# A turn of a quarter in place of a squared half angle: h·cos h between two matmuls, with the order of tasks written anew

## Chip, cores and metric

One core of one Trainium2 chip. The time is device microseconds of one execution; 929.7 us is the median of three runs of the kernel before (925.52 to 930.39).

## What is computed

Attention over 4 batches, 8 heads, 576 positions, head size 64: softmax attention on q, k, v averaged by fours, repeated four times, plus softmax attention within a band of |i-j| < 4. Its output x, 2304 rows of 512, goes through two multilayer products:

```
h = x @ w_in          # 512 -> 2048
g = h * cos(h)
y = g @ w_out         # 2048 -> 512
out = ((y @ w_a) * (y @ w_b)) @ w_out2   # 512 -> 1536 -> 512
```

All inputs are float32 (some arrive as 64-bit words and are converted on the core). Each factor of a large product is split into a rounded part and the rest, and a product is three matmuls: high·high, high·low, low·high (`mm3`, L577 to L579).

## The kernel before

Tokens are cut into 8 units of 288 for attention and into 7 stretches (five of 288 columns, two of 432) for the first product pair. A **group** g is one stretch with one of the 16 blocks of 128 hidden features; there are 112. Per group: `h{g}.0..3` (four `mm3` of x with w_in into one of two PSUM banks called `h`), `c{g}.0..6` (the cosine, function `cosine`, L624 to L645), `b{g}.0..3` (four `mm3` with w_out into `acc0` to `acc3`). Because the banks number two, a group's first matmul waits until the group two places earlier in the order has left its bank. That happens at the step that multiplies by h, L639.

The cosine before, per group: ScalarE rounds h/2π to an integer (L628), VectorE subtracts that many turns from h (L630), ScalarE takes the sine of half the rest (L632), ScalarE (L635) or VectorE (L637) squares it and doubles it, VectorE forms (1 - that)·h (L639). Then follow a rounded copy `gh` (L293 or L295) and the rest `gl` (L645), which the back matmuls read.

All of this and the attention (`sm` to `xl`: scores L384 and L408, maxima, exponentials L430/L437/L440, sums, transposes L476/L489, products L504/L511, the sum of both parts L527, the split into `xbig` L293/L295/L551) and the conversion of weights (`w{t}.0..4`: ScalarE L276 and L279, VectorE L281, copy L293/L295, rest L570) is written in one string, `ORDER`. A word such as `c5.1@d` is a task and its engine (a ScalarE, d VectorE, p GpSimd); each engine's instructions, and the queue of loads, run in the order of that string. ScalarE has one function table for exponentials and one for sines; a change is an ACT_TABLE_LOAD. After the string come the last products (`z`, L577 to L579 too), whose order is made by loops that the change leaves alone.

Of the kernel before, what the change touches and what calls it, by code (L numbers as in the profile page):

```python
# [48 lines left out]
L0w7 w7.0@a w7.1@a xl0.1@p h1.0 h1.1 h0.1 ln0.1 lz0.1@d L0s3 vs0.3@d L0w5 vs0.2@p L0w6 dt0.1 w4.4@p w3.1@a w3.2@d dc0.1@a w3.3@d lt0.1 lc0.10@a
lc0.11@a at0.1 Lc8 w5.0@a w5.1@a w5.2@d up0.1@a cb0.3 Lc13 w6.1@a w3.4@p cb0.2 xh0.3@a xh0.2@d xl0.2@d xl0.3@d w6.0@a w6.2@d lp1.0 w8.0@a Lq1.3 w5.3@a  # L50
w7.2@d w5.4@p h0.2 h0.3 c0.0@a c0.1@d w6.3@a h1.2 h1.3 c1.0@a lm1.0 Lc9 w6.4@p c0.2@a c0.3@a c1.1@d c1.2@a w7.3@d lu1.0@p dp1.0 c0.4@d c0.5@d h2.0
h2.1 h2.2 lu1.1@p w8.1@a c1.3@a h2.3 dx1.0 da1.00@d c0.6@p b0.1 Lq1.2 c1.4@d c1.5@d h3.0 h3.1 h3.2 h3.3 da1.01@d b0.0 w9.0@a w8.2@d lp1.1 sm1.3@d b0.3
w8.3@d b0.2 sm1.2@p c1.6@p b1.2 b1.3 b1.1 le1.0 ln1.0 Lc14 c2.0@a c2.1@d b1.0 lm1.1 Lc11 w11.0@a c3.0@a de1.0 c3.1@d w9.1@a w9.2@d w8.4@p dp1.1 dn1.0
lz1.0@p lu1.2@p Lq2.2 c2.2@a c2.3@a c3.2@a c2.4@d Lc10 w10.0@a dx1.1 da1.10@d h4.0 h4.1 da1.11@d dz1.1@p lu1.3@p Lc22 c2.5@a c2.6@p c3.3@a c3.4@d
c3.5@d h4.2 h4.3 w11.1@a w7.4@d dz1.0@p w10.1@a Lw2.0 lt1.0 lc1.00@d w9.3@d Lc27 c4.0@a c4.1@d lc1.01@d w10.2@d b2.2 Lc21 de1.1 b2.1 w11.2@d c3.6@p
dn1.1 w11.3@d Lq2.0 h5.0 h5.1 h5.2 Lk2.1 h5.3 c5.0@a c5.1@d L0V le1.1 ln1.1 dt1.0 b2.0 Lc12 w10.3@d w9.4@p b2.3 dc1.0@a at1.0 up1.0@d cb1.0 cb1.1
# [1164 lines left out]
```

## Time and profile before

| | |
|---|---|
| median of three runs | 929.7 us (925.52 to 930.39) |
| the profiled execution | 928.92 us, span 927.1 us |
| busy: TensorE, VectorE, ScalarE, GpSimd | 891.7, 705.2, 576.2, 509.2 us |
| mean granted TensorE clock | 0.987 |

PE is TensorE's matmuls, PEld its weight loads, DVE VectorE, ACT ScalarE, POOL GpSimd. A row of groups names line, engine, operation, tile written and tiles read, shapes, count, then busy time and mean of one in ns, then the idle time of the engine just before and what ended it. A matmul's end is modelled, so its row is longer than the step to the next one.

### The profile page before, as it was taken

The page shows a single profiled execution, that of the slowest core. Times are in us where ns is not written, and L with a number is a line of the kernel's source. Part 1 is how long each engine was busy: PE and PEld are TensorE (multiplying, and loading weights), DVE is VectorE, ACT ScalarE, POOL GpSimd, SP SyncE. Part 2 cuts the span into 40 slices and gives each one's busy share as a digit, 9 for nine tenths or more (in the row PEclk, how much of TensorE's full clock was granted, in tenths as well). Part 3 has the DMA queues.
Part 4 walks back from the last instruction along what each step waited for, and adds up shares of the span by engine and source line. Part 5 has one row for each costly group of instructions (what it writes and reads, how often), then busy time and mean ns, then how long its engine had stood idle before and what let it go on. Part 6 is the DMA issues. An engine that isn't in the chain of part 4 may idle for free.

```text
span 927.1 us, 18811 instructions
## 1 busy us (share of the span) xinstructions
PE 891.7 (96%) x6828; PEld 864.4 (93%) x6828; DVE 705.2 (76%) x1332; ACT 576.2 (62%) x1249; POOL 509.2 (55%) x654
## 2 busy tenths in 40 slices
PE   4688999999999999999999999999999999999998
PEld 2588999999999999999998999999999999999998
DVE  6899998797687876855666697869768677776764
ACT  5797988566486785743575555557644566544473
POOL 4566766455166655631545177656576753677540
PEclk9788999999999999999999999999999999999999
DMA  9775432254475755400787454594743366832641
GB/s 260 249 262 183 144 122 84 79 152 134 146 226 156 233 164 175 144 1 24 227 288 204 147 199 156 177 384 183 281 176 112 106 236 244 333 105 72 219 160 52
DMA packets 97581, 162.12 MB, mean 175 GB/s; under 512 B 6736, under 2 KB 63568, under 8 KB 97488
## 3 DMA queue, kind: packets, MB, share of 16 engines
q1 hardware_dynamic: 97488, 160.92, 52.3%
q8 instruction: 54, 0.88, 0.4%
q14 instruction: 39, 0.32, 0.1%
HBM read 127.66 MB, written 33.23 MB: 174 GB/s over the span
## 4 chain that ended last, share of the span: by engine, by line
PE 81%; DVE 10%; ACT 3%; issue 3%; POOL 2%; DMA 0%; SPq 0%; POOLq 0%; DVEq 0%; ACTq 0%
PE z L578 14%; PE z L577 14%; PE z L579 14%; PE acc L577 6%; PE h L577 6%; PE acc L578 6%; PE acc L579 6%; PE h L579 5%; PE h L578 5%; DVE raw L281 1%; PE att L384 1%; DVE gs L639 1%; PE att L511 1%; PE att L476 1%; PE att L504 1%
## 5 line engine op out<-in xcount | busy, mean ns | idle before, releaser
L968 POOL TENSOR_TENSOR sb<-w,sb 128x256 fp32r<-128x256 f32 x154 | 125.2, 826 | 115.5 <-ACT sb L966 110.5
L577 PE MATMUL h<-xbig,w 128*128 128x288 f32 (+1 forms) x448 | 147.0, 328 | 8.4 <-DVE gs L639 8.3
L577 PE MATMUL acc<-gh,w 128*128 128x288 f32 (+1 forms) x448 | 144.1, 322 | 0.0
L579 PE MATMUL h<-xbig,w 128*128 128x288 f32 (+1 forms) x448 | 142.2, 317 | 0.0
L578 PE MATMUL h<-xbig,w 128*128 128x288 f32 (+1 forms) x448 | 141.9, 317 | 0.0
L578 PE MATMUL acc<-gl,w 128*128 128x288 f32 (+1 forms) x448 | 141.0, 315 | 0.7 <-DVE gl L645 0.7
L579 PE MATMUL acc<-gh,w 128*128 128x288 f32 (+1 forms) x448 | 140.8, 314 | 0.0
L966 ACT ACTIVATE sb<-w 128x256 fp32r<-128x256 f32 x252 | 97.0, 415 | 53.0 <-PE z L579 44.3
L577 PEld LDWEIGHTS h<-xbig,w 128*128 128x128 f32 x448 | 86.2, 192 | 14.2 <-DVE gs L639 11.2
L645 POOL TENSOR_TENSOR gl<-gs,gh 128x288 fp32r<-128x288 f32 (+1 forms) x61 | 59.4, 980 | 69.9 <-ACT gh L293 35.0
L577 PE MATMUL z<-xbig,sb 128*128 128x384 f32 x288 | 97.3, 338 | 0.0
L579 PE MATMUL z<-xbig,sb 128*128 128x384 f32 x288 | 97.2, 337 | 0.0
L578 PE MATMUL z<-xbig,sb 128*128 128x384 f32 x288 | 97.1, 337 | 0.0
L628 ACT ACTIVATE gs<-h 128x288 int32<-128x288 f32 (+1 forms) x112 | 49.4, 441 | 64.5 <-PE h L579 60.3
L577 PEld LDWEIGHTS acc<-gh,w 128*128 128x128 f32 x448 | 85.0, 190 | 3.6 <-issue 1.2
L579 PEld LDWEIGHTS h<-xbig,w 128*128 128x128 f32 x448 | 86.3, 193 | 1.0
L578 PEld LDWEIGHTS h<-xbig,w 128*128 128x128 f32 x448 | 86.2, 192 | 1.0
L578 PEld LDWEIGHTS acc<-gl,w 128*128 128x128 f32 x448 | 85.0, 190 | 1.9 <-DVE gl L645 0.9
L579 PEld LDWEIGHTS acc<-gh,w 128*128 128x128 f32 x448 | 84.9, 190 | 1.0
L630 DVE SCALAR_TENSOR_TENSOR gs<-gs,h 128x288 f32<-128x288 int32 (+1 forms) x112 | 54.9, 491 | 37.0 <-ACT gs L628 36.7
L632 ACT ACTIVATE gs<-gs 128x288 f32<-128x288 f32 (+1 forms) x112 | 53.3, 477 | 40.6 <-DVE gs L630 40.0
L968 DVE TENSOR_TENSOR sb<-w,sb 128x256 fp32r<-128x256 f32 x98 | 60.6, 620 | 22.8 <-ACT sb L966 22.6
(160 smaller groups left out, 2451.7 us busy)
## 6 DMA issues: line engine op xcount, KB each, us to landing
w<-wd SPq DMA_DIRECT2D x63, 512.0 KB
w<-wd_a SPq DMA_DIRECT2D x18, 512.0 KB
w<-wd_b SPq DMA_DIRECT2D x18, 512.0 KB
raw<-in_w_in_dram SPq DMA_DIRECT2D x16, 512.0 KB
raw<-in_w_out_dram SPq DMA_DIRECT2D x16, 512.0 KB
w<-wd_a SPq DMA_DIRECT2D x18, 384.0 KB
w<-wd_b SPq DMA_DIRECT2D x18, 384.0 KB
praw<-in_w_a_dram SPq DMA_DIRECT2D x12, 512.0 KB
```

Of the source, the lines that this page charges most:

```text
L281: dve.scalar_tensor_tensor(out=lw if out is None else out, in0=hh, scalar=3, in1=lw, op0=ALU.logical_shift_left, op1=ALU.bitwise_or)
L384: pe.matmul(p[i][o, W * w:W * w + W], qt[u, 2 * pr + i][r, off:off + W], kt[u // 2, 2 * pr + i][r, BASE[half] + off:BASE[half] + off + W], ...
L476: pe.transpose(p[part][:, 128 * i:128 * i + 128], pt[u, pr][:, s], ident)
L577: i = pe.matmul(ps_out, lh, rh, start=start, stop=False, skip_group_check=more)
L578: pe.matmul(ps_out, lh, rl, start=False, stop=False, skip_group_check=more)
L579: pe.matmul(ps_out, ll, rh, start=False, stop=stop, skip_group_check=more)
L628: act.activation(out=gs[g].bitcast(I32), in_=hps[g], func=AF.Copy, scale=1.0 / (2.0 * math.pi))
L630: dve.scalar_tensor_tensor(out=gs[g], in0=gs[g].bitcast(I32), scalar=-2.0 * math.pi, in1=hps[g], op0=ALU.mult, op1=ALU.add)
L632: act.activation(out=gs[g], in_=gs[g], func=AF.Sin, scale=0.5)
L645: eng.tensor_tensor(out=gl[g], in0=gs.pop(g), in1=gh[g].bitcast(F32), op=ALU.subtract)
L966: act.activation(out=t[:, 0], in_=blk, func=AF.Copy)
L968: (dve if nst[0] % (C["SD"] if G else C["SD0"]) == 0 else pool).tensor_tensor(out=t[:, 1], in0=blk, in1=t[:, 0].bitcast(F32), op=ALU.subtract)
```

## The change

The integer is rounded from h/2π + 1/4 (the quarter comes as a bias from a column of a small tile `turn`), the rest is h minus those turns, the sine is taken of the rest plus π/2 (a bias from another column), and VectorE multiplies it by h. The step that squares is gone; the steps after it are renumbered (`c{g}.0..5`). The column `down`, used in L279, moves into `turn`. `ORDER` is written anew: 112 words fewer, the rest in another order and partly on other engines. Lines after the string lie 6 lower, and those after the cosine 11 lower; then 8.

```diff
-            act.activation(out=gs[g].bitcast(I32), in_=hps[g], func=AF.Copy, scale=1.0 / (2.0 * math.pi))
+            act.activation(out=gs[g].bitcast(I32), in_=hps[g], func=AF.Identity, scale=1.0 / (2.0 * math.pi), bias=turn[:, 0:1])
         elif stage_ == 1:
             dve.scalar_tensor_tensor(out=gs[g], in0=gs[g].bitcast(I32), scalar=-2.0 * math.pi, in1=hps[g], op0=ALU.mult, op1=ALU.add)
         elif stage_ == 2:
-            act.activation(out=gs[g], in_=gs[g], func=AF.Sin, scale=0.5)
+            act.activation(out=gs[g], in_=gs[g], func=AF.Sin, bias=turn[:, 1:2])
         elif stage_ == 3:
-            if eng is act:
-                act.activation(out=gs[g], in_=gs[g], func=AF.Square, scale=math.sqrt(2.0))
-            else:
-                eng.scalar_tensor_tensor(out=gs[g], in0=gs[g], scalar=2.0, in1=gs[g], op0=ALU.mult, op1=ALU.mult)
+            dve.tensor_tensor(out=gs[g], in0=gs[g], in1=hps[g], op=ALU.mult)
         elif stage_ == 4:
-            dve.scalar_tensor_tensor(out=gs[g], in0=gs[g], scalar=1.0, in1=hps[g], op0=ALU.subtract, op1=ALU.mult, reverse0=True)
-        elif stage_ == 5:
...
-    down = const.tile([128, 1], F32, name="down")
+    turn = const.tile([128, 3], F32, name="turn")
+    dve.memset(turn[:, 0:1], 0.25)
+    dve.memset(turn[:, 1:2], math.pi / 2.0)
+    down = turn[:, 2:3]
...
-        for k in range(7):
+        for k in range(6):
```

Two lines of the string as a sample, of before and now; `c36` has seven steps there and six here:

```
-vs4.5@p S31.2 da4.01@d b32.0 c36.2@a c36.3@a c35.6@p c36.4@d sm4.3@d b32.1 b33.3 c36.5@a p0.0 p0.10 h37.0 h37.1 h37.2 h37.3 b33.1 b34.1 b35.1
+c36.1@d c36.2@a b32.3 b32.1 da4.01@d S31.2 S31.3 c35.4@d b33.3 b34.3 p0.0 p0.10 h37.0 c36.3@d c35.5@d p0.11 h37.1 h37.2 p1.0 p0.12 p0.2 h37.3 c37.0@a
```

**Place 1, ScalarE at the first two cosines, before** (`gs_532` and `gs_543` are their tiles, `h_375` and `h_397` the two banks):

```order
L628 ACTIVATE gs_532<-h_375 128x288
L293 ACTIVATE w_535<-raw_423 128x512
L628 ACTIVATE gs_543<-h_397 128x288
L632 ACT_TABLE_LOAD
L632 ACTIVATE gs_532<-gs_532 128x288
L635 ACTIVATE gs_532<-gs_532 128x288
L632 ACTIVATE gs_543<-gs_543 128x288
L279 ACTIVATE raw_478<-raw_478,down_100 128x512
L635 ACTIVATE gs_543<-gs_543 128x288
```

and in the changed kernel (`gs_534` first, `gs_553` second; L622 rounds, L626 is the sine):

```order
L622 ACTIVATE gs_534<-h_375,turn_100 128x288
L287 ACTIVATE w_537<-raw_434 128x512
L626 ACT_TABLE_LOAD
L626 ACTIVATE gs_534<-gs_534,turn_100 128x288
L622 ACTIVATE gs_553<-h_371,turn_100 128x288
L270 ACTIVATE raw_532<-raw_532 128x512
L273 ACTIVATE raw_532<-raw_532,turn_100 128x512
L626 ACTIVATE gs_553<-gs_553,turn_100 128x288
```

The table load now stands ahead of the second group's rounding, and the second group's sine stands behind a weight conversion.

**Place 2, VectorE at the same point, before** (L639 frees a bank):

```order
L630 SCALAR_TENSOR_TENSOR gs_532<-gs_532,h_375 128x288
L391 TENSOR_TENSOR smx_545<-att_498,mask_79 128x2x5x64
L396 TENSOR_REDUCE mx_547<-smx_545 128x10
L630 SCALAR_TENSOR_TENSOR gs_543<-gs_543,h_397 128x288
L295 CAST w_556<-raw_392 128x512
L639 SCALAR_TENSOR_TENSOR gs_532<-gs_532,h_375 128x288
```

and in the changed kernel (L624 subtracts the turns, L628 multiplies by h):

```order
L624 SCALAR_TENSOR_TENSOR gs_534<-gs_534,h_375 128x288
L385 TENSOR_TENSOR smx_540<-att_489,mask_79 128x2x5x64
L390 TENSOR_REDUCE mx_542<-smx_540 128x10
L628 TENSOR_TENSOR gs_534<-gs_534,h_375 128x288
L624 SCALAR_TENSOR_TENSOR gs_553<-gs_553,h_371 128x288
```

The first bank's release has moved ahead of the second group's subtraction and of a weight's copy.

**Place 3, TensorE at groups 35 to 37 of the changed kernel** (`h_2692` is group 36, `h_2706` group 35, `h_2798` group 37, which takes the bank of 36):

```order
L571 MATMUL h_2706<-xbig_82,w_1649 128x288
...
L571 MATMUL h_2692<-xbig_82,w_2008 128x288
...
L571 MATMUL acc_2776<-gh_2721,w_1592 128x288
...
L571 MATMUL acc_2776<-gh_2750,w_1778 128x288
...
L571 MATMUL h_2798<-xbig_82,w_1922 128x288
```

Between the last matmul of group 36 and the first of group 37 stand four `mm3` of back work, twelve matmuls. Before, group 37 took the bank of group 35, and between these two stood group 36 whole and six `mm3` of back work.

## Rows read from the trace of the kernel before

**Rows 1.** Page, part 1: busy time and share of each engine.
```profile
PE 891.7 (96%) x6828; PEld 864.4 (93%) x6828; DVE 705.2 (76%) x1332; ACT 576.2 (62%) x1249; POOL 509.2 (55%) x654
```
**Rows 2.** Busy time of each engine by stretch (us), granted clock, DMA share, GB/s.
```profile
0.00:45.00 45.00, 23.76 (x306) 19.32 (x306) 34.59 (x63) 28.57 (x70) 22.74 (x36) 0.85 0.83 251
45.00:90.00 45.00, 38.68 (x446) 36.02 (x449) 41.79 (x80) 37.59 (x83) 30.68 (x37) 0.89 0.66 233
90.00:150.00 60.00, 58.32 (x622) 54.91 (x614) 56.85 (x114) 52.21 (x107) 37.39 (x40) 1.00 0.39 123
510.00:900.00 390.00, 390.00 (x2215) 389.39 (x2214) 296.24 (x529) 216.88 (x518) 237.75 (x263) 1.00 0.54 194
```
**Rows 3.** Waits of TensorE, 45 to 92 us: total, times, longest.
```profile
PE h L577 <- DVE gs L639: 4.9, 3, 2.4
PE att L476 <- POOL smx L450: 1.9, 1, 1.9
```
**Rows 4.** Waits of TensorE, 90 to 510 us.
```profile
PE h L577 <- DVE gs L639: 3.4, 5, 1.0
PE acc L578 <- DVE gl L645: 0.7, 1, 0.7
```
**Rows 5.** TensorE in order of time: start, duration; two steps at each clock.
```profile
46.74 0.29 PE L578 MATMUL h<-xbig,w 128*128 128x288 f32 x1
46.87 0.29 PE L579 MATMUL h<-xbig,w 128*128 128x288 f32 x1
...
49.06 0.45 PE L577 MATMUL h<-xbig,w 128*128 128x288 f32 x1
49.30 0.45 PE L578 MATMUL h<-xbig,w 128*128 128x288 f32 x1
```
**Rows 6.** Groups by shape, cosine, whole span; then the squares of 0 to 90 us.
```profile
L628 ACT ACTIVATE gs<-h 128x288 int32<-128x288 f32 x80 | 32.5, 406 | 34.7 <-PE h L579 31.6 <-POOL w L570 1.2 <-POOL gl L645 1.0
L632 ACT ACTIVATE gs<-gs 128x288 f32<-128x288 f32 x80 | 35.2, 441 | 22.7 <-DVE gs L630 22.5
L635 ACT ACTIVATE gs<-gs 128x288 f32<-128x288 f32 x59 | 25.9, 441 | 1.2
L635 ACT ACTIVATE gs<-gs 128x432 f32<-128x432 f32 x17 | 9.6, 562 | 0.4
L637 DVE SCALAR_TENSOR_TENSOR gs<-gs 128x288 f32<-128x288 f32 x21 | 11.8, 561 | 3.9 <-ACT gs L632 3.7
L637 DVE SCALAR_TENSOR_TENSOR gs<-gs 128x432 f32<-128x432 f32 x15 | 9.2, 614 | 5.9 <-ACT gs L632 5.7
L639 DVE SCALAR_TENSOR_TENSOR gs<-gs,h 128x288 f32<-128x288 f32 x80 | 35.6, 446 | 7.4 <-ACT gs L635 6.7
L635 ACT ACTIVATE gs<-gs 128x288 f32<-128x288 f32 x8 | 3.5, 434 | 0.1
```
**Rows 7.** Groups by shape: the nearest rows for the new forms.
```profile
L276 ACT ACTIVATE raw<-raw 128x512 f32<-128x512 f32 x32 | 21.1, 672 | 6.8 <-DMA raw<-in_w_in_dram 6.8
L279 ACT ACTIVATE raw<-raw,down 128x512 uint32<-128x512 uint8 x32 | 24.0, 765 | 0.0
L527 DVE TENSOR_TENSOR xf<-att,xf 128x288 f32<-128x288 f32 x32 | 13.1, 448 | 3.8 <-ACT xf L293 3.5
```
**Rows 8.** ScalarE, VectorE, TensorE in order of time at the first cosine.
```profile
41.08 0.41 ACT L628 ACTIVATE gs<-h 128x288 int32<-128x288 f32 x1 [1.41 <-PE h L579]
41.39 0.67 ACT L293 ACTIVATE w<-raw 128x512 fp32r<-128x512 f32 x1
42.52 0.41 ACT L628 ACTIVATE gs<-h 128x288 int32<-128x288 f32 x1 [0.47 <-PE h L579]
42.95 1.28 ACT L632 ACT_TABLE_LOAD   x1
45.20 0.46 DVE L639 SCALAR_TENSOR_TENSOR gs<-gs,h 128x288 f32<-128x288 f32 x1 [0.48 <-ACT gs L635]
45.70 0.40 PE L577 MATMUL h<-xbig,w 128*128 128x288 f32 x1 [1.79 <-DVE gs L639]
```

More of the change, by code (lines that the diff above doesn't have):

```diff
@@ L49 @@
[L49 to L56, printed above, removed]
@@ L173 @@
[L173 to L175 removed]
+L0q0 L0k0 sm0.0@d L0q1 L0k1 lp0.0 L0q2 sm0.1@d dp0.0 L0w1 lm0.0 lu0.1@d L0s0 lu0.0@d w1.1@a w1.0@a w1.2@d dx0.0 da0.01@d da0.00@d L0w0 le0.0 ln0.0
+lz0.0@d lt0.0 w0.0@a de0.0 dn0.0 w0.1@a L0q3 w0.2@d L0k2 sm0.2@d dz0.0@a L0s1 w1.3@a vs0.0@p dz0.1@p dt0.0 L0k3 sm0.3@d dp0.1 lc0.00@a w0.3@a w1.4@d
@@ new lines @@
+dx0.1 vs0.1@p L0w2 dc0.0@a w2.0@a lc0.01@d w2.1@a w2.2@d w0.4@d L0v at0.0 L0w4 L0s2 da0.10@d up0.0@d cb0.0 cb0.1 da0.11@a w2.3@a w2.4@p xh0.0@d
+xl0.0@p de0.1 dn0.1 xh0.1@a xl0.1@p lp0.1 lm0.1 lu0.3@d lu0.2@d dz0.3@a dz0.2@a w4.0@a w4.1@a w4.2@d h1.0 h0.0 h0.1 le0.1 ln0.1 L0w3 h1.1 dt0.1
+dc0.1@a L0s3 vs0.3@d w4.3@a L0w7 Lq1.0 w3.0@a L0w5 w3.1@a w3.2@d w4.4@d vs0.2@p w7.1@a w7.0@a w7.2@d lz0.1@p lt0.1 L0w6 lc0.10@a lc0.11@a at0.1
+sm1.0@d up0.1@d cb0.2 w3.3@a w3.4@p cb0.3 w5.0@a w5.1@a w6.1@a xh0.2@d w5.2@d xl0.2@d xh0.3@a xl0.3@d w6.0@a w6.2@d Lq1.1 lp1.0 w7.3@a Lc11 w11.1@a
@@ new lines @@
+b14.1 Lc28 c15.3@d w26.0@a w19.3@a w21.1@a w24.1@a w19.4@p up2.1@d cb2.3 b14.2 h16.1 cb2.2 h17.0 xh2.2@d xl2.2@d w26.1@a c15.4@a xh2.3@a w27.1@a
+c15.5@d b12.3 xl2.3@d b13.3 sm3.0@d w26.2@d h17.1 h17.2 h17.3 w21.0@a c17.0@a w22.3@d w22.4@p h16.2 h16.3 c17.1@d b15.2 c16.0@a c17.2@a c16.1@d
+c17.3@d w23.0@a c16.2@a w30.1@a w25.2@d b14.3 b15.3 w24.2@d b14.0 c16.3@d c17.4@a lp3.0 lm3.0 w20.4@p c17.5@p h18.0 e15.3@a h18.1 h18.2 h18.3 w24.3@a
+c16.4@d Lk4.1 Lq4.1 c16.5@p w27.0@a h19.0 h19.1 h19.2 c18.0@a c18.1@d w30.0@a Lk4.3 h19.3 Lq3.3 e15.2@d S15.2 b15.1 c18.2@a c18.3@d c19.0@a w17.3@d
@@ new lines @@
+b81.0 b81.3 b82.3 c85.0@a c85.1@d dz7.3@d dz7.0@d b81.2 p23.11 b82.2 le7.1 lz7.0@p c85.2@a dz7.1@d p23.10 b82.0 c84.4@d c84.5@p lt7.0 lc7.00@a
+lc7.01@a c85.3@d c85.4@d p23.12 h86.2 h86.3 h87.0 c85.5@d c86.0@a c86.1@d c86.2@a c86.3@d b83.3 dt7.0 dc7.0@d h87.1 h87.2 p22.5 b82.1 b83.1 h87.3
+ln7.1 lz7.1@d h89.0 c87.0@a p24.0 p24.10 c87.1@d c87.2@a c86.4@a c87.3@d at7.0 h89.1 h89.2 p24.11 b83.0 h89.3 up7.0@d cb7.1 xh7.1@d b83.2 b84.2 cb7.0
+xh7.0@d dz7.2@p h88.0 p23.2 c89.0@a c89.1@d lt7.1 h88.1 h88.2 h88.3 c89.2@a c89.3@d b85.2 b84.3 c87.4@d c87.5@d S79.2 p24.12 p24.2 b84.1 lc7.10@a
@@ L176 @@
+b105.1 b106.1 b106.0 b105.3 b107.0 b106.2 b107.2 c111.0@a c111.1@d c111.2@a c111.3@d c109.4@d c109.5@d x12.5 b106.3 b107.3 b107.1 b108.1 c111.4@d
+c111.5@d b108.2 c110.4@d c110.5@d F14 F15 b109.2 b110.2 b111.2 e111.2@d S111.2 b108.3 b109.3 b110.3 b111.3 e111.3@d S111.3 b109.1 b110.1 b111.1
+e111.1@d b108.0 b109.0 b110.0 b111.0 e111.0@d S111.1 S111.0
 """
@@ L278, in to_f32 @@
             top = raw.rearrange("p f e -> p (f e)").bitcast(mybir.dt.uint8).rearrange("p (f b) -> p f b", b=8)[:, :, 3]
-            act.activation(out=lw, in_=top, func=AF.Identity, scale=1.0 / 32.0, bias=down[:, :1])
+            act.activation(out=lw, in_=top, func=AF.Identity, scale=1.0 / 32.0, bias=down)
         if 2 in stages:
```

230 lines of the change are left out of this document (107 added, 123 removed).

## The prediction

> **What bounds the kernel now.** I read the share of busy time first, then the same by stretch, then who waited for whom on TensorE, then single instructions. TensorE is busy for 891.7 of 927.1 us [rows 1], so at most 35 us of it are idle, and any gain must come from these or from time at a low clock. By stretch [rows 2] the idle time lies at the start: TensorE is busy 23.8 of the first 45 us and 38.7 of the next 45, then 58.3 of 60, and from 510 to 900 us without a gap. The clock was granted in full from 90 us on, and at a mean of 0.85 and 0.89 in the first two stretches. A matmul of 288 columns starts every 0.13 us at the full clock and every 0.24 us at the lower one [rows 5], which is 1.2 against 2.4 GHz. So a mean of 0.89 over 45 us is about 10 us at the low level, and these cost some 4 to 5 us of the work done in them.
>
> In those first 90 us VectorE is the fullest of the others: 34.6 of 45, then 41.8 of 45 us; ScalarE has 28.6 and 37.6 [rows 2]. What TensorE waits for there is the reader's main row: 4.9 us in three waits for VectorE's last cosine step, L639, which frees a bank, and 1.9 us for GpSimd's scaling of the scores [rows 3]. Behind 90 us the same wait is there five times, 3.4 us in all, none over 1.0, and once 0.7 us for `gl` [rows 4]. The reader should see from this that the cosine matters as a delay, at eight places, and that its cost in busy time matters only ahead of 90 us, where ScalarE and VectorE are nearly full.
>
> **What the change removes.** 112 squares. On ScalarE 59 take 25.9 us and 17 take 9.6; on VectorE 21 take 11.8 and 15 take 9.2 [rows 6]. That is 35.5 and 21.0 us of busy time. Nearly all of it lies beside a full TensorE, and costs nothing there. Of the squares only eight of ScalarE fall in the first 90 us, 3.5 us [rows 6]; the order puts one more on VectorE there, 0.56 us by its mean.
>
> **What it adds.** A bias read from a column of a tile, in two ScalarE passes per group, 224 in all. No pass of the cosine has one now. Its price lies between nothing and 0.093 us: the two passes over one weight tile of 128x512 take 0.672 us without and 0.765 us with such a bias [rows 7], but they also differ in the type that they read, so the difference need not be the bias alone. It can't be below nothing, as the rounding and the sine stay the same passes over the same elements. I take 0.093, as these are the same engine and the same tile. ScalarE then gets back 35.5 - 20.8 = 14.7 us, and in the first 90 us, with nine or ten groups, 3.5 - 1.8 = 1.7 us. The Trainium skill speaks against the change here: "ScalarE: Activation LUTs", section on what ACT_TABLE_LOAD costs, states that each operand that is a pointer to one value per partition adds about 93 ns to an ACTIVATE. By that rule the upper end holds; with the lower one the sum below would be 1.5 us better. The row's difference agrees with it.
>
> The new multiplication by h, two inputs of which one lies in PSUM, is like L527, 0.448 us for 288 columns, where L639 takes 0.446 [rows 6, 7]: no difference. The two extra memsets stand at the start, where ScalarE has no weight yet to convert, and cost nothing; were VectorE late there, two passes as long as L527 would be 0.9 us, which the range keeps.
>
> **What it does to the delay.** Before, a 288-column bank is held for L628 0.406, L630 (taken as L639, 0.45), L632 0.441, the square 0.441 and L639 0.446, 2.2 us and five handovers [rows 6]. Now it is 0.50 + 0.45 + 0.53 + 0.45 = 1.93 us and four. The saving is 0.441 - 0.186 = 0.26 us behind a square of ScalarE, 0.561 - 0.186 = 0.38 behind one of VectorE, and a handover of some 0.04 us (L639 ends at 45.66 and the matmul starts at 45.70 [rows 8]): 0.3 to 0.4 us.
>
> **What it moves, and the sum.** (1) First bank, places 1 and 2. Now L628 starts at 41.08, then comes a copy of a weight, then L628 of the second group, which itself waits 0.47 us for TensorE, then the table load at 42.95, the sine, the square, and L639 at 45.20; the third group's first matmul starts at 45.70 after 1.79 us idle [rows 8]. In the new order the table load doesn't stand behind the second group's rounding. From 41.08: rounding 0.50 to 41.58, copy to 42.15, table load 1.28 to 43.45, sine 0.53 to 43.98, multiplication 0.45 to 44.45, against 45.66. That is **1.2 us** less of the wait of 1.79. (2) The other two waits of that kind ahead of 90 us, 4.9 - 1.8 = 3.1 us, get shorter by 0.35 each: **0.7 us**. (3) The five behind 90 us would lose 0.35 each, 1.7 us together. But the new order sets groups nearer to each other. At place 3 group 37 takes the bank of group 36, and only twelve matmuls at 0.13, 1.6 us, stand between, where the chain needs 1.93 us and four handovers, some 2.1: a new wait of 0.5 us. I count two such places, and keep **0.7 us**. (4) 1.7 us of relief on ScalarE and 0.56 on VectorE in a stretch where both are full: I let half of it reach TensorE, **1.0 us**. Its other end is nothing, since some of VectorE's new work (pieces that GpSimd did, such as the second subtraction of maxima in unit 0) eats what is freed. (5) Behind 510 us nothing is changed, and TensorE has no gap to close: 0.
>
> Sum: 1.2 + 0.7 + 0.7 + 1.0 = 3.6 us. The profiled execution took 928.92 us, 0.8 below the median of the runs shown, 929.7; against it the sum is **925.3 us**.
>
> **Rivals.**
> *The opening comes loose.* The waits of rows 3 are 6.8 us, of which the sum takes 1.9 (and 1.0 more as relief); what is left is 3.9 us. The low clock of that stretch costs 4 to 5 us. The rows show one such piece: the steps are at the low level at 49.06, shortly behind the gap that ends at 45.70 [rows 5, 8], so fewer gaps may give more of the full clock. If both go: 928.9 - 3.6 - 3.9 - 4.5 = 916.9; half of it, 921. For it: VectorE and ScalarE lose work just there. Against it: 2.3 us of relief in 90.
>
> *The opening gets later (the other side).* The new order gives VectorE more of the early attention. Counting its instructions ahead of the release of each of the first four banks, by the durations of rows, I come to 1.3 to 2.2 us more than before, an estimate. VectorE is the fullest there [rows 2]. If it decides, groups 2 to 5 start up to 2.2 us later, and two further idle stretches each bring a piece at the low clock, about 1.7 us each (the 10 us at the low level, over the three waits for L639 of rows 3, are 3.4 us each, of which half is lost): 928.9 + 2.2 + 3.4 - 0.7 = 933.8. It decides where the third group's first matmul starts behind 46.5 us. Against it: by hand the opening chain reaches that point a little sooner.
>
> *The gain is spent.* The waits behind 90 us come back in number as fast as they shrink, and the opening is bound by loads and weight conversion, which are the same: 0 to 1.5 us gained, 928.5.
>
> **How the numbers follow.** Forecast 0.40, opening loose 0.25, opening later 0.17, gain spent 0.18. A measurement of this kernel can tell about 0.5% (4.65 us) from no change. The forecast, taken with its bounds (2 to 5.5 us gained), is beyond that in a third of its cases, the loose opening nearly always: 0.13 + 0.23 = 0.36 for faster. The later opening is beyond it in two cases of three, and I add 0.04 for a wait in the new order that I haven't seen: 0.16 for slower. The rest, 0.48, is no difference that can be told. As faster and same hold most of the chance, the forecast's own range is 923.4 to 927. The range that holds 8 in 10 reaches from the deeper half of the loose opening to the later one: 917 to 934.
>
> **What would show it.** In the profile after, L635 and L637 are gone, the rounding is near 0.50 and the sine near 0.53 us at 288 columns; near 0.41 and 0.44 the price of the bias was wrong. The third group starts near 44.5 us. TensorE's waits for the last cosine step add up to 5 to 6 us instead of 8.3. From 510 us on the stretch of products is as long as before. I am wrong if the idle time ahead of 90 us changes by more than 4 us either way, if a wait for `gl` or for a load shows up behind 90 us with more than 2 us, or if the products take longer.

## The result, and the profile after

| | before | after |
|---|---|---|
| median | 929.4 us (925.52 to 930.39, 4 runs) | 918.7 us (918.41 to 919.23, 4 runs) |
| profiled execution, its span | 928.92, 927.1 us | 918.41, 916.6 us |

The ratio is 0.9893, 95% interval 0.9864 to 0.9922: faster by 10.7 us. The forecast, 925.3, stood 4.4 under the median shown and 3.6 under the profiled execution; the measured time is 6.6 under the forecast. It is inside the range and nearest to the rival that lets the opening come loose, 916.9.

Busy time on the page of the changed kernel, against [rows 1]:
```profile
PE 886.7 (97%) x6828; PEld 861.0 (94%) x6828; DVE 691.9 (75%) x1312; ACT 567.8 (62%) x1188; POOL 479.0 (52%) x618
```
Its stretches, with the columns of [rows 2]:
```profile
0.00:45.00 45.00, 25.04 (x319) 21.18 (x319) 35.59 (x76) 31.03 (x68) 20.49 (x31) 0.89 0.78 255
45.00:90.00 45.00, 40.99 (x501) 37.22 (x502) 43.04 (x86) 42.03 (x88) 28.83 (x36) 1.00 0.72 253
90.00:150.00 60.00, 58.95 (x609) 56.44 (x608) 55.22 (x112) 53.80 (x108) 34.28 (x34) 1.00 0.35 111
510.00:900.00 390.00, 390.00 (x2221) 389.79 (x2220) 294.77 (x525) 218.51 (x518) 234.78 (x259) 1.00 0.53 190
```
TensorE is busy for more of both early stretches and has the full clock from 45 us on, where it had 0.89. VectorE and ScalarE are no emptier there than before: they do more in the same time. TensorE's idle time ahead of 90 us fell from 27.6 to 24.0 us. The products are a full stretch as before.

Waits of TensorE in the changed kernel, 45 to 92 us and then 90 to 510, against [rows 3, 4]:
```profile
PE h L571 <- DVE gs L628: 2.2, 3, 1.2
PE h L573 <- DVE w L564: 1.0, 1, 1.0
...
PE h L571 <- DVE gs L628: 1.4, 2, 0.9
PE att L483 <- DVE smx L289: 0.9, 1, 0.9
```
Groups by shape, against [rows 6]:
```profile
L626 ACT ACTIVATE gs<-gs,turn 128x288 f32<-128x288 f32 x80 | 42.7, 535 | 23.0 <-DVE gs L624 22.3
L622 ACT ACTIVATE gs<-h,turn 128x288 int32<-128x288 f32 x80 | 39.5, 494 | 30.6 <-PE h L573 26.9 <-issue 1.2 <-DVE gl L634 0.8
L628 DVE TENSOR_TENSOR gs<-gs,h 128x288 f32<-128x288 f32 x80 | 35.9, 450 | 18.0 <-ACT gs L626 17.6
```
The rounding takes 0.494 us (forecast 0.50), the sine 0.535 (0.53), the multiplication 0.450 (0.448). TensorE's waits for the last cosine step come to 4.6 us in the whole span (forecast 5 to 6).

The changed kernel in order of time at the first cosine, against [rows 8]:
```profile
39.23 0.50 ACT L622 ACTIVATE gs<-h,turn 128x288 int32<-128x288 f32 x1 [0.88 <-PE h L573]
40.32 1.28 ACT L626 ACT_TABLE_LOAD   x1
41.61 0.53 ACT L626 ACTIVATE gs<-gs,turn 128x288 f32<-128x288 f32 x1
42.18 0.46 DVE L628 TENSOR_TENSOR gs<-gs,h 128x288 f32<-128x288 f32 x1 [0.38 <-ACT gs L626]
42.69 0.40 PE L571 MATMUL h<-xbig,w 128*128 128x288 f32 x1 [0.97 <-DVE gs L628]
```
From the first rounding to the third group's first matmul it takes 42.69 - 39.23 = 3.46 us, before 45.70 - 41.08 = 4.62. The third group starts at 42.69 us, where 44.5 was forecast. But the rounding itself also starts 1.85 us sooner. The third stretch of local scores, ahead of any cosine, shows the same 1.85 (before, then the change):
```profile
37.96 1.35 PE L384 MATMUL att<-k,q 64*64 64x64 f32 x40 [1.51 <-ACT xbig L293]
```
```profile
36.11 1.35 PE L378 MATMUL att<-k,q 64*64 64x64 f32 x40 [1.33 <-issue]
```
The first of the last products starts 10.6 us sooner (before, then the change):
```profile
525.63 0.34 PE L577 MATMUL z<-xbig,sb 128*128 128x384 f32 x1
```
```profile
515.04 0.34 PE L571 MATMUL z<-xbig,sb 128*128 128x384 f32 x1
```
To see where in between it is gained, I weighted each matmul of both traces by its step at the full clock, summed them up, and compared the times at which both kernels reach the same sum. As the orders differ and some records are missing, this is good to about half a microsecond.

| stretch (times of before) | the change is ahead by, at its end | gained in it |
|---|---|---|
| to the third scores, 38 us (from the rows) | 1.85 us | 1.85 |
| to the third group, 45.7 us (from the rows) | 3.0 | 1.15 |
| to 77.5 us | 4.5 | 1.5 |
| 77.5 to 87 us | 8.2 | 3.7 |
| 87 to 462 us | 8.0 | -0.2 |
| to the first last product (from the rows) | 10.6 | 2.6 |

So a third of the gain falls within ten microseconds around 80 us, and nothing in the 375 us behind them.

### The profile page after: what moved, and what is told of

The parts are those of the page before. It is cut to its first block, busy times and chain, and to the rows that moved or that the text cites. A ratio compares the mean times of both kernels' runs of the same rounds, so it can differ in the third digit from the quotient of the medians.

```text
span 916.6 us, 18718 instructions
## 1 busy us (share of the span) xinstructions
PE 886.7 (97%) x6828; PEld 861.0 (94%) x6828; DVE 691.9 (75%) x1312; ACT 567.8 (62%) x1188; POOL 479.0 (52%) x618
## 4 chain that ended last, share of the span: by engine, by line
PE 87%; DVE 5%; DMA 3%; ACT 3%; issue 1%; POOL 1%; SPq 0%; ACTq 0%; POOLq 0%; DVEq 0%
PE z L571 14%; PE z L573 14%; PE z L572 14%; PE h L571 7%; PE acc L571 7%; PE acc L573 6%; PE acc L572 6%; PE h L573 6%; PE h L572 6%; DMA raw<-in_w_in_dram 2%; PE att L505 1%; PE att L498 1%; DVE raw L275 1%; PE att L470 1%; PE att L378 1%
## 5 line engine op out<-in xcount | busy, mean ns | idle before, releaser
L634 POOL TENSOR_TENSOR gl<-gs,gh 128x288 fp32r<-128x288 f32 (+1 forms) x55 | 55.1, 1002 | 95.9 <-ACT gh L287 49.6
L622 ACT ACTIVATE gs<-h,turn 128x288 int32<-128x288 f32 (+1 forms) x112 | 59.3, 529 | 59.1 <-PE h L573 48.8
L571 PEld LDWEIGHTS h<-xbig,w 128*128 128x128 f32 x448 | 85.3, 190 | 9.7 <-DVE gs L628 6.5
L626 ACT ACTIVATE gs<-gs,turn 128x288 f32<-128x288 f32 (+1 forms) x112 | 63.7, 570 | 42.1 <-DVE gs L624 41.0
L573 PEld LDWEIGHTS h<-xbig,w 128*128 128x128 f32 x448 | 85.2, 190 | 2.3 <-DVE w L564 1.3
L572 PEld LDWEIGHTS h<-xbig,w 128*128 128x128 f32 x448 | 85.4, 191 | 1.4 <-POOL xbig L545 0.4
L624 DVE SCALAR_TENSOR_TENSOR gs<-gs,h 128x288 f32<-128x288 int32 (+1 forms) x112 | 55.0, 491 | 35.5 <-ACT gs L622 34.1
L628 DVE TENSOR_TENSOR gs<-gs,h 128x288 f32<-128x288 f32 (+1 forms) x112 | 55.2, 494 | 34.6 <-ACT gs L626 34.0
```

The source lines that it names most:

```text
L571: i = pe.matmul(ps_out, lh, rh, start=start, stop=False, skip_group_check=more)
L572: pe.matmul(ps_out, lh, rl, start=False, stop=False, skip_group_check=more)
L573: pe.matmul(ps_out, ll, rh, start=False, stop=stop, skip_group_check=more)
L622: act.activation(out=gs[g].bitcast(I32), in_=hps[g], func=AF.Identity, scale=1.0 / (2.0 * math.pi), bias=turn[:, 0:1])
L624: dve.scalar_tensor_tensor(out=gs[g], in0=gs[g].bitcast(I32), scalar=-2.0 * math.pi, in1=hps[g], op0=ALU.mult, op1=ALU.add)
L626: act.activation(out=gs[g], in_=gs[g], func=AF.Sin, bias=turn[:, 1:2])
```

## The experiments

Unless said otherwise a median stands against the 918.7 us of the change. Kernels 2 to 7, 10 and 11 run their matmuls in the order of the change, kernel 8 from 50 us on (all but for a few swaps between 479 and 509 us), and kernels 1, 9 and 12 in that of before; there "ahead" and "behind" are told by the start of one and the same matmul in both profiled executions, at a time of the change (of before for kernel 12). Kernels 1 to 4 ran together (before 929.4 us), then 5 to 8 (930.1), 9 to 11 (926.8), and 12 (929.5). The runs of before lie in two bunches, at 924.3 to 927.2 and 928.2 to 931.6 us; how many fall in each moves its median, which is why the medians of the variants are compared with each other. The shortest runs of before in these four sets, 924.3, 925.8, 925.4 and 925.0 us, lie 1.5 us apart, so a smaller difference between kernels of different sets says little.

**1. The old order with the new cosine.** The old string, its squares dropped, the rest renumbered (first line of the string):
```diff
-L0q0 L0k0 sm0.0@d L0q1 L0k1 lp0.0 L0q2 sm0.1@d dp0.0 L0w1 lm0.0 lu0.1@d L0s0 lu0.0@d w1.1@a w1.0@a w1.2@d dx0.0 da0.01@d da0.00@d L0w0 le0.0 ln0.0
+L0k0 L0q0 sm0.0@d L0k1 L0q1 lp0.0 lm0.0 lu0.0@d L0w1 w1.0@a w1.1@a sm0.1@p dp0.0 dx0.0 da0.01@d w1.2@d L0q2 L0k2 sm0.2@d lu0.1@p le0.0 ln0.0 L0s0
```


> The new cosine with the order of before: the words of the squares are taken out of the old string, the later steps renumbered, nothing else moved. Theory A (the order made the gain; the removed step alone is worth what the prediction's terms 2 to 4 say): 926 to 929 us, TensorE's waits for the last cosine step 6 to 8 us in all, the low clock ahead of 90 us about as long as before. Theory B (the removed step made the gain, in any order): 918 to 922 us, the three waits between 478 and 504 us gone, and fewer pieces at the low clock.

Measured 925.4 us (919.95 to 926.42), ratio to before 0.9959 (0.9936 to 0.9983). The time lies between the theories, nearer to A. Its rows are nearer to B: the waits for the last cosine step are 4.3 us in all, one of the three late ones is left (0.45 us at 496.6), and no stretch at the low clock lies between 45.2 and 90 us. But the profiled execution, 921.26 us, is one of the two shortest of ten.

**2. The new order with the old cosine.** Each square stands right behind its sine (ScalarE) or right ahead of its product (VectorE); the cosine is that of before. One line of the string:
```diff
-c36.1@d c36.2@a b32.3 b32.1 da4.01@d S31.2 S31.3 c35.4@d b33.3 b34.3 p0.0 p0.10 h37.0 c36.3@d c35.5@d p0.11 h37.1 h37.2 p1.0 p0.12 p0.2 h37.3 c37.0@a
+c36.0@a c36.1@d c36.2@a c36.3@a b32.3 b32.1 da4.01@d S31.2 S31.3 c35.5@d b33.3 b34.3 p0.0 p0.10 h37.0 c36.4@d c35.6@d p0.11 h37.1 h37.2 p1.0 p0.12
```


> The old cosine with the order of the change: each square is put back right behind its sine on ScalarE, or right ahead of the product on VectorE, on the engine that it had before; nothing else moved. Theory A (order): 919 to 924 us, the opening up to 45 us within 1.5 us of the change's. Theory B (removed step): 927 us or more, since the new order sets groups nearer and each is released 0.3 to 0.4 us later; TensorE's waits for the last cosine step then add up to 8 us or more.

Measured 937.4 us (936.57 to 937.64), ratio to before 1.010 (1.0063 to 1.0138): theory B holds, though the opening is only 0.7 us behind the change at 43 us. TensorE's wait for the last cosine step in the whole span, 8.3 us in 8 waits before and 4.6 in 6 after, is here:
```profile
PE h L577 <- DVE gs L639: 10.4, 12, 2.1
```
What follows from both: removing the square is worth 4.0 us in the old order (929.4 - 925.4) and 18.7 in the new one (937.4 - 918.7). The order without the removal loses 8.0. Kernel 1 lies in two bunches as before does; bunch against bunch (925.5 against 930.5, 920.6 against 925.8) the removal is worth about 5 in the old order. Neither part has a price of its own. My reading is that the new order sets groups as close as the shorter chain allows.

**3. Biases written as constants** in the two ScalarE passes, in place of columns of a tile.
```diff
-func=AF.Identity, scale=1.0 / (2.0 * math.pi), bias=turn[:, 0:1])
+func=AF.Copy, scale=1.0 / (2.0 * math.pi), bias=0.25)
...
-func=AF.Sin, bias=turn[:, 1:2])
+func=AF.Sin, bias=math.pi / 2.0)
```


> The change with both biases as constants in the instruction in place of a column of a tile (Copy with 0.25, Sin with pi/2): if the column costs 0.093 us a pass, the rounding falls from 0.494 to about 0.40 us and the sine from 0.535 to about 0.44 us at 288 columns, ScalarE's busy time falls by about 20 us, and the time by 0.5 to 2 us (six waits of 4.6 us get shorter by up to 0.19 each, and the full ScalarE ahead of 90 us gets 1.8 us back). If the column costs nothing, no row and no time moves.

Measured 916.9 us (916.3 to 917.23), ratio to before 0.988 (0.9844 to 0.9917): better than both kernels. Its groups by shape:
```profile
L626 ACT ACTIVATE gs<-gs 128x288 f32<-128x288 f32 x80 | 35.3, 442 | 25.3 <-DVE gs L624 25.0
L622 ACT ACTIVATE gs<-h 128x288 int32<-128x288 f32 x80 | 32.3, 403 | 37.7 <-PE h L573 32.1 <-issue 1.5 <-DVE gl L634 1.3
```
0.494 - 0.403 = 0.091 and 0.535 - 0.442 = 0.093 us: that is the price of a bias from a column, with the type and the elements the same.

**4. More matmuls in an early gap.** Forty transposes of the identity ahead of `lt0.1`, into columns that nobody reads.
```diff
+        if (u, pr) == (0, 1):
+            for n in range(40):
+                pe.transpose(p[n % 2][:QD, 288 + 72 * (n % 3):360 + 72 * (n % 3)], ident[:QD, :QD], ident[:QD, :QD])
```


> The change with 40 transposes that nothing reads, between the down-sampled and the local transposes of the first unit, where TensorE sits idle for 3.4 us ahead of 31 us; they write columns of the same bank that no one uses. If the low clock from 30 to 40 us comes from that idle stretch, the clock stays full there, the scores and first groups behind 31 us run at 0.13 in place of 0.24 us a step, the third group starts 1 to 3 us sooner, and the time falls by 1 to 3 us. If the low clock there has another cause, or the chain of that stretch is VectorE's and ScalarE's alone, the time stays within 0.7 us of the change.

Measured 921.0 us (919.36 to 922.78): slower, where 1 to 3 us less was one expectation and no change the other. The low clock starts at 33.15 instead of 29.95 us and ends at 39.98 instead of 40.2, and a second such piece stands at 43.4 to 46.8. Nothing of it reaches the work that counts: without the added transposes TensorE is 0.2 us behind the change at 31 us, 0.8 at 34, 1.6 at 46 and 0.8 again at 60. The third group starts at 43.50 us, 0.8 later. It is 0.9 behind at 494 us, and 1.3 more come at one wait, at 499.1 us (1.07), which is taken up below.

**5 and 6. ScalarE loaded.** Two short passes behind each sine, for groups 0 to 9 (kernel 5) or 10 to 111 (kernel 6). Nothing reads them.
```diff
+            for k in range(2 if g < 10 else 0):
+                act.activation(out=turn[:, 4:7], in_=turn[:, 0:3], func=AF.Square)
...
-    turn = const.tile([128, 3], F32, name="turn")
+    turn = const.tile([128, 8], F32, name="turn")
```


> The changed kernel, with two passes of ScalarE that do nothing of use behind the sine of each of the first ten groups (three columns of a small tile to three others, 0.20 us each by the one such pass at the kernel's start): ScalarE gets 10 x 0.41 = 4.1 us more ahead of 90 us, about what the squares were there; the chain of a group stays short, since nobody waits for these passes. If the gain ahead of 90 us came from the relief of a full ScalarE (term 4 of the prediction), the time goes back by 2 to 4 us, to 921 to 923. If it came from the shorter chain, it stays within 1 us of the changed kernel's 918.7, to 919.7 at the most. Theory: the chain.

Measured 923.9 us (923.64 to 924.42). My theory fell: a load on ScalarE counts. A pass takes 0.198 us, so the load is 4.0 us. The kernel is 0.9 us behind the change at 38 us, ahead of the first added pass, 2.9 at 84 us, 3.3 at 400 and 5.6 at 510. So 2.1 us are what the load cost by 84 us, when 18 of the 20 passes have run (3.5 us); 1.0 of it falls in two pieces at the low clock (43.5 to 46.9 and 64.0 to 67.4 us) that the change doesn't have. The last 2.3 come late, 1.7 of them at one wait. What a load costs doesn't say what relief brings; kernels 3 and 10 are nearer to that.

> The same two passes in groups 10 to 111 (102 groups, 204 passes, 41 us of ScalarE), nearly all of them behind 90 us. If busy time of ScalarE beside a full TensorE is free, as the prediction held for the squares: 918 to 920. If the changed kernel's gain behind 90 us (about 3 us, the three late waits) is ScalarE's free time: 921 or more.

Measured 924.5 us (922.5 to 925.36): the rival holds. The profiled execution, the shortest of the five, is 1.7 us ahead of the change at 89 us, 0.9 behind at 170, 1.5 at 494 and 4.1 from 510 on. So 2.6 us are lost between 89 and 170 us. Its row for 90 to 150 us, where the change has 58.95 of TensorE and 53.80 of ScalarE:
```profile
90.00:150.00 60.00, 57.67 (x592) 54.31 (x591) 53.74 (x108) 56.73 (x137) 31.69 (x31) 1.00 0.35 108
```
From 170 to 494 us the passes cost 0.6 us. The last 2.6 come by 510 us, most of them at a wait for `gl` at 499.2 us (0.75) and one for `gh` at 510.9 (0.88).

**7. The old cosine behind group 9.** The change, with the old four steps and the square for g >= 10.
```diff
+    OLD = lambda g: g >= 10
...
+            if OLD(g):
+                act.activation(out=gs[g], in_=gs[g], func=AF.Sin, scale=0.5)
...
+        elif stage_ == 9:
+            if eng is act:
+                act.activation(out=gs[g], in_=gs[g], func=AF.Square, scale=math.sqrt(2.0))
```


> The changed kernel with the old cosine (rounding and sine without a bias, a square right behind the sine or right ahead of the product) in groups 10 to 111 alone. The first ten groups are as in the change. The new order with the old cosine everywhere lost 14 us behind 90 us against the change, in waits for the last cosine step. If the chain's length there is what costs, this loses 10 to 16 us: 929 to 935, with eight or so waits for the last cosine step behind 90 us, 6 to 8 us in all. If the loss of that kernel was mostly what its late opening left behind, this comes to 921 to 924.

Measured 934.4 us (932.45 to 934.86), 15.7 over the change. The waits for the last cosine step behind 90 us, 1.4 us in two there, are here:
```profile
PE h L576 <- DVE gs L646: 7.2, 9, 2.1
```
ScalarE's load alone doesn't make this: kernel 6 had 40 us of load and lost 5.8, and the 102 groups here have some 70 squares on ScalarE, less the price of 204 biases, which is under 20. Step by step against the change, 6.1 us of the loss stand right at waits for the last cosine step and 4.3 at waits for `gh`, `gl` and the softmax. So the longer chain with VectorE's share of the squares makes the larger part; the two weren't tried apart.

**8. The old opening.** The old string to the release of the second bank (`c1.3@d`), then the new one. The lines at the seam:
```diff
-h2.2 dx1.0 c0.4@d h2.3 w8.1@a w8.2@d c1.2@a c1.3@d da1.00@d da1.01@d Lq1.2 c1.4@d Lq1.3 w8.3@d le1.0 ln1.0 c0.5@p Lc9 Lk2.0 de1.0 dn1.0 h3.0 h3.1 b0.2
...
+lu1.1@p w8.1@a h2.3 dx1.0 da1.00@d c0.5@p b0.1 Lq1.2 c1.3@d Lc11 w11.1@a w8.2@d da1.01@d c1.4@d w8.3@d le1.0 ln1.0 Lk2.0 de1.0 dn1.0 h3.0 h3.1 b0.2
```


> The new cosine with the old string (without its squares) up to the release of the second bank, and the new string from there. At equal work of TensorE the change was 3 us ahead of the old string with the new cosine at 46 us. If the order of the opening makes that and it is kept: 921 to 922. If it is swallowed later by the wait for the next stage: 918 to 919.5.

Measured 923.1 us (920.93 to 923.59), 4.4 over the change: the opening is kept, and is worth more than the 3 us that I read. It is 3.2 us behind at 43 (by the sums), 4.0 at 84 and 4.1 at 494 us.

**9. The new opening.** The new string to the same word, the old one behind it.
```diff
-h2.2 dx1.0 c0.4@d h2.3 w8.1@a w8.2@d c1.2@a c1.3@d da1.00@d da1.01@d Lq1.2 c1.4@d Lq1.3 w8.3@d le1.0 ln1.0 c0.5@p Lc9 Lk2.0 de1.0 dn1.0 h3.0 h3.1 b0.2
+h2.2 dx1.0 c0.4@d h2.3 w8.1@a w8.2@d c1.2@a c1.3@d Lc13 Lq1.3 Lc9 da1.00@d c0.5@p b0.1 Lq1.2 c1.4@d h3.0 h3.1 h3.2 h3.3 da1.01@d b0.0 w9.0@a lp1.1
```


> The new cosine with the new string up to the release of the second bank, and the old string (without its squares) from there: the mirror of the kernel with the old opening, which came to 923.1, 4.4 us behind the change; the old string throughout came to 925.4. If the opening and the rest add up, this is 925.4 - 4.4 = 921.0, between 920 and 922. If the new opening pays only with what the new order does behind it, it stays at 924 to 926.

Measured 921.7 us, inside the range for opening and rest that add up. But two of the seven runs took 917.3, the other five 921.4 to 923.3. Two bunches with middles some 5 us apart are also in before and in kernel 1 (919.95 and 921.26, then 924.61 to 926.42). Bunch against bunch, kernel 9 is 3.0 to 3.3 us under kernel 1. All three hold the old order behind the opening.

**10. No bias from a column at all.** Kernel 3, and L273 with its bias as a constant.
```diff
-            act.activation(out=lw, in_=top, func=AF.Identity, scale=1.0 / 32.0, bias=down)
+            act.activation(out=lw, in_=top, func=AF.Copy, scale=1.0 / 32.0, bias=-31.0 / 64.0)
```


> The kernel with plain biases (916.9), and the third bias that is read from a column, that of the weights' second pass, written as a constant too: 32 passes of 0.765 us should come to 0.672, 20 of them ahead of 92 us, 1.9 us less of ScalarE there. Ten groups with 4.1 us more of ScalarE ahead of 90 us cost 3.6 us at 84 us and 5.2 in all. If ScalarE's busy time there is the bound, both ways, this gains 1.5 to 2.5 us: 914.4 to 915.4. If loading ScalarE costs but relieving it doesn't, since VectorE is next: within 0.7 us of 916.9.

Measured 916.4 us (915.42 to 916.95), the shortest of all. The pass came down from 0.765 to 0.670 us, but the median is only 0.5 under that of kernel 3, and the two sets of runs overlap. More relief of ScalarE doesn't bring what a load costs.

**11. The old order of the early attention.** The old string to the third scores (`lp1.0`), then the new one. The lines at the seam:
```diff
-sm1.0@d up0.1@d cb0.2 w3.3@a w3.4@p cb0.3 w5.0@a w5.1@a w6.1@a xh0.2@d w5.2@d xl0.2@d xh0.3@a xl0.3@d w6.0@a w6.2@d Lq1.1 lp1.0 w7.3@a Lc11 w11.1@a
...
+lc0.11@a at0.1 Lc8 w5.0@a w5.1@a w5.2@d up0.1@a cb0.3 Lc13 w6.1@a w3.4@p cb0.2 xh0.3@a xh0.2@d xl0.2@d xl0.3@d w6.0@a w6.2@d lp1.0 w7.2@d w7.3@a Lc11
```


> The new cosine with the old string up to the third stretch of local scores (the matmuls that start at 37.96 us before and at 36.11 us in the change), and the new string from there, so that the order at the first two cosines is the new one. Before, the third group starts 7.7 us behind those scores, in the change 6.6. If the order of the attention ahead of the cosines makes the early part (1.9 us of 3.0) and the order at the cosines the rest, the third group starts near 44.5 us and the kernel takes 920.5 to 921.5. If it is the cosines' order alone: 918.5 to 919.5; if the attention's alone: 922.5 to 923.5.

Measured 922.1 us (920.72 to 923.45), between the first case and that of the attention alone. The third group starts at 45.86 us, not 44.5: the scores came at 38.83, and 7.03 us passed from there, where I expected 6.6. From the second piece of the first scores (6.0 to 7.2 us) to the third scores it takes 31.3 to 32.2 us in the five kernels with the old attention and 29.0 to 30.8 in the nine with the new one. Which of its words do this wasn't tried, but the traces show what differs. Ahead of the third scores VectorE is busy in before and in the change for:
```profile
0.00:37.96 37.96, 18.09 (x246) 14.46 (x247) 29.15 (x54) 23.46 (x62) 18.48 (x32) 0.90 0.86 260
```
```profile
0.00:36.11 36.11, 18.03 (x247) 14.99 (x247) 28.00 (x60) 23.07 (x56) 15.47 (x26) 0.91 0.80 259
```
The change has six passes more there and yet 1.15 us less. At their usual lengths its passes would take 1.5 us more; but in before seven passes, each of them begun while a GpSimd pass ran, are 3.8 us longer than usual in all (3.8 to 4.2 in the five kernels with the old attention), and in the change three are 1.3 us longer (1.3 to 1.9 in the nine). The two longest of before, whose kinds otherwise take 0.17 and 0.68 us:
```profile
30.18 1.00 DVE L445 TENSOR_SCALAR sl<-sl 128x10 f32<-128x10 f32 x1
35.43 1.70 DVE L281 SCALAR_TENSOR_TENSOR raw<-raw 128x512 uint32<-128x512 uint32 x1 [0.22 <-ACT raw L279]
```
Kernel 12 tries such a place, later in the kernel.

**12. One pass of VectorE moved, in the kernel before.** What may part the bunches shows in two traces. In before VectorE's copy rest L551 starts 0.14 us behind a GpSimd pass and takes 1.49 us; 2.5 us later L281 starts 0.10 behind another one and takes 1.26; the last cosine step comes late, and TensorE waits 2.39 us. Rows of GpSimd, VectorE and TensorE of before:
```profile
74.34 1.31 POOL L570 TENSOR_TENSOR w<-raw,w 128x512 fp32r<-128x512 f32 x1 [1.36 <-ACT w L293]
74.48 1.49 DVE L551 TENSOR_TENSOR xbig<-xf,xbig 128x288 fp32r<-128x288 f32 x1
76.89 0.80 POOL L551 TENSOR_TENSOR xbig<-xf,xbig 128x288 fp32r<-128x288 f32 x1 [1.24 <-ACT xbig L293]
76.99 1.26 DVE L281 SCALAR_TENSOR_TENSOR raw<-raw 128x512 uint32<-128x512 uint32 x1
80.10 0.45 DVE L639 SCALAR_TENSOR_TENSOR gs<-gs,h 128x288 f32<-128x288 f32 x1
80.60 0.40 PE L577 MATMUL h<-xbig,w 128*128 128x288 f32 x1 [2.39 <-DVE gs L639]
```
Kernel 9, profiled in its upper bunch (922.75 us), has 1.51, 1.26 and a wait of 2.38 us at that place; kernel 1, profiled in its lower one (921.26), has 0.54, 0.71 and 0.76. The edit, the word `xl1.0@d` put ahead of `sm2.0@d` (two lines of the string):
```diff
-c4.5@d lc1.10@d dz1.3@p w11.4@d Lk2.0 w12.1@a w12.2@d b3.1 c4.6@p Lc15 w15.1@a w14.1@a dt1.1 dc1.1@d w14.2@d h7.0 h7.1 h7.2 at1.1 sm2.0@d w12.3@a
-w12.4@p b3.3 b4.3 xl1.0@d w13.1@a h7.3 w14.3@a Lc19 b3.2 up1.1@a cb1.2 cb1.3 w14.4@p c6.0@a b4.2 Lq2.1 c6.1@d Lc18 w13.0@a w13.2@d c5.5@a b4.0 c5.6@d
+c4.5@d lc1.10@d dz1.3@p w11.4@d Lk2.0 w12.1@a w12.2@d b3.1 c4.6@p Lc15 w15.1@a w14.1@a dt1.1 dc1.1@d w14.2@d h7.0 h7.1 h7.2 at1.1 xl1.0@d sm2.0@d
+w12.3@a w12.4@p b3.3 b4.3 w13.1@a h7.3 w14.3@a Lc19 b3.2 up1.1@a cb1.2 cb1.3 w14.4@p c6.0@a b4.2 Lq2.1 c6.1@d Lc18 w13.0@a w13.2@d c5.5@a b4.0 c5.6@d
```


> The kernel before, whose runs so far lie at 924 to 926 or at 928 to 931, with one pass of VectorE moved: L551 for the second unit, which starts at 74.48 us beside a GpSimd pass that started at 74.34 and takes 1.49 us in place of 0.54, goes ahead of the two L361 that stand in front of it; nothing else changes on any engine. Theory: two passes that collide by 0.14 us cost TensorE a wait of 2.4 us at 80 us and, behind it, a piece at half the clock; that is the upper of the two levels, and it is 3 to 4 us of the 10.7. Then every run lies at 924 to 927, the median near 925.5, the wait near 80 us is about 0.9, and no low clock follows it. Rival: the collision is not what parts the levels; then the runs still lie at both, with a median of 927 to 930.

Measured 926.7 us, 12 runs, all at 925.04 to 927.45; before beside it 929.5 (4 of 17 runs at 925.0 to 926.0, the other 13 at 928.2 to 931.6). The ratio is 0.9976 (0.996 to 0.9993). The upper bunch is gone, and the theory holds, though the median lies 1.2 us over the 925.5 expected and a few runs a little over 927. Rows of kernel 12 at that place:
```profile
73.42 0.44 DVE L551 TENSOR_TENSOR xbig<-xf,xbig 128x288 fp32r<-128x288 f32 x1
75.90 0.68 DVE L281 SCALAR_TENSOR_TENSOR raw<-raw 128x512 uint32<-128x512 uint32 x1
78.47 0.43 DVE L639 SCALAR_TENSOR_TENSOR gs<-gs,h 128x288 f32<-128x288 f32 x1
78.96 0.40 PE L577 MATMUL h<-xbig,w 128*128 128x288 f32 x1 [0.93 <-DVE gs L639]
```
L551 and L281 are 1.05 and 0.58 us shorter, 1.63 together, and L639 comes 80.10 - 78.47 = 1.63 us sooner. Kernel 12 is 0.15 us ahead of before at 77 us, 1.64 behind the wait, 3.18 at 85 and 2.75 at the end. So the wait makes 1.5 us, and another 1.5 is the clock. The stretch behind the wait, in before and in kernel 12 (columns as in [rows 2]):
```profile
81.00:85.00 4.00, 4.00 (x20) 4.00 (x20) 3.94 (x8) 2.34 (x6) 3.77 (x6) 0.57 0.86 285
```
```profile
79.00:83.00 4.00, 4.00 (x33) 3.64 (x33) 3.97 (x7) 3.11 (x7) 3.92 (x5) 1.00 0.75 229
```

## Why the prediction came out too small

**Removal and its price: right.** The bias costs 0.091 and 0.093 us, taken at 0.093; the new forms cost what was said, and behind 510 us nothing moved.

**Term 1, the first bank, 1.2 us: right in size, not all there is.** From the first rounding to the third group the change gained 4.62 - 3.46 = 1.16 us. From the third scores to the third group it takes 7.74 us before, 7.27 with the old opening and the new cosine (kernel 8), 6.87 with the new order and the old cosine (kernel 2), 6.58 in the change: by single traces the order at these places gives 0.7 to 0.9, the removal 0.3 to 0.5. (Kernel 6, which is the change up to group 9, has 5.57, so this split isn't firm.) What the sum lacked is the **attention ahead of it**, 1.85 us. I had counted VectorE's instructions there and put the new order 1.3 to 2.2 us later, as a rival. The count was right, 1.5 us more at usual lengths, and the sign of the outcome wrong: it left out that VectorE's passes get longer beside GpSimd's, by 3.8 us before and by 1.3 in the change (under kernel 11; read from the traces, not tried there). Kernels 8 and 9 show that the opening as a whole is worth 3 to 4 us; kernel 11, that most of it stands ahead of the third scores.

**Term 2, the other early waits, 0.7 us: the step that failed.** I took the wait of 2.4 us at 80.6 as one for the chain's length, and gave it 0.35. Its cause was a collision between VectorE and GpSimd, and the wait itself brought a piece of low clock. Both are gone in the change, since its order sets these passes otherwise; 3.7 us of the 10.6 fell there. Kernel 12 removes them in the kernel before, by moving a single pass and without touching the cosine: 2.8 us of the median, 3.0 at the place. So more than a quarter of the change's gain needs no other cosine; it comes from the order.

**Term 3, the waits behind 90 us, 0.7 us: wrong in place.** Up to 462 us nothing came, and the 2.6 us came mostly from three waits for the last cosine step at 479.9, 496.7 and 504.4 us (0.54, 0.66, 0.97) that the change doesn't have. In before, from 470 to 510 us:
```profile
PE h L577 <- DVE gs L639: 2.2, 3, 1.0
```
Kernel 1 has one of them left, with 0.45, so the shorter chain takes most of it in the old order too. The waits that I set against this never came: there is none at place 3. There I read the banks wrongly. These rows of ScalarE, VectorE and TensorE in the change show group 35 rounded at 183.93 and multiplied at 186.64, then group 37 begin, and only then group 36 multiplied, at 188.09: group 37 takes the bank of 35, not that of 36 as the text on place 3 has it.
```profile
183.93 0.50 ACT L622 ACTIVATE gs<-h,turn 128x288 int32<-128x288 f32 x1 [0.41 <-PE h L573]
186.64 0.45 DVE L628 TENSOR_TENSOR gs<-gs,h 128x288 f32<-128x288 f32 x1
187.24 0.32 PE L571 MATMUL h<-xbig,w 128*128 128x288 f32 x1
188.09 0.46 DVE L628 TENSOR_TENSOR gs<-gs,h 128x288 f32<-128x288 f32 x1
```
**Term 4, relief, 1.0 us: not shown.** Kernel 5 gives the price of a load, some 0.6 us for one of ScalarE. Relief is measured by kernel 3, which takes some 1.8 us off ScalarE ahead of 90 us and shortens the chain as well: it is 0.4 us ahead of the change at 89 us. The 1.5 us that the table has between 45.7 and 77.5 us can't be put down to relief, since before has two pieces at the low clock there (47.1 to 50.5 and 67.6 to 71.0 us) and the change none. And "nearly all of it lies beside a full TensorE, and costs nothing there" doesn't hold: kernel 6 lost 2.6 us between 89 and 170 us, and as much again behind 494.

**The rivals.** The opening did come loose: the rival had 12.0 us off the profiled execution, the result is 10.5. That the range held is in part luck: the rival's two halves, waits and clock, both went, but its reason, relief of ScalarE and VectorE, is not the one that the runs bear out. Nor is the tie between them firm: kernels 2 and 7 both wait 2.10 us for the last cosine step, at 159.3 and 155.9 us, and the low clock follows in kernel 2 (159.6 to 163.0) and not in kernel 7. Its price for the clock must be read with care. In kernel 12 the piece of 3.4 us was worth 3.18 - 1.64 = 1.5, a little under half its length, as the prediction priced it. But kernel 3 has such a piece at 61.7 to 65.1 us, falls by it from 0.4 us ahead of the change to 1.1 behind, and is ahead by 0.4 again at 75 us: at 65.9 the change waits 1.0 us for `w`, and kernel 3 doesn't. And the profiled execution of kernel 7 has the highest mean clock of all, 0.998, and is 14.0 us longer than that of the change. So a low clock costs little where TensorE would have waited anyway.

**What stays open.** That every run of before in the upper bunch had the collision is seen in the profiled one alone, and follows for the others only from their going with it. The clock doesn't part the bunches throughout: of the 36 upper runs of before beside kernels 1 to 12, 28 have a mean clock of 0.985 to 0.989, under the 0.990 to 0.992 of the 18 lower ones, but eight, at 929.0 to 930.7 us, have 0.994. What holds those eight back isn't known. Why kernels 4, 5 and 8 have a late wait that the change lacks is seen in kernel 5 but wasn't tried. There VectorE is second by 0.5 us, and its passes take 1.48 and 1.41 us:
```profile
496.88 1.55 POOL L636 TENSOR_TENSOR gl<-gs,gh 128x432 fp32r<-128x432 f32 x1 [10.35 <-ACT gh L287]
497.36 1.48 DVE L885 TENSOR_TENSOR xw<-xb,xw 128x384 fp32r<-128x384 f32 x1
498.76 1.41 DVE L636 TENSOR_TENSOR gl<-gs,gh 128x432 fp32r<-128x432 f32 x1
502.54 0.46 PE L571 MATMUL h<-xbig,w 128*128 128x432 f32 x1 [1.41 <-DVE gs L630]
```
In the change the same GpSimd pass came while VectorE was at work, and it was GpSimd that lost (2.10 us), which nobody waited for:
```profile
492.95 2.10 POOL L634 TENSOR_TENSOR gl<-gs,gh 128x432 fp32r<-128x432 f32 x1 [11.24 <-ACT gh L287]
493.00 0.60 DVE L634 TENSOR_TENSOR gl<-gs,gh 128x432 fp32r<-128x432 f32 x1
```

## What to carry to other kernels

Before a wait is put down to the length of the chain behind it, look along the chain for a pass that takes two or three times its usual time, and at what GpSimd does beside it: moving one such pass gave 3 us here. Count such losses too when an engine's work is added up by the usual lengths of its passes. A change that comes with a new order should be split both ways (new order with old code, old order with new code, and the order cut at a point), since the removal was worth 4 to 5 us in one order and 19 in the other. Where a constant will do as a bias, write the constant: it saved 0.09 us a pass and made the change better by 1.8 us.
